# A spectral and MLP kernel on one core: group 0 normalized three quarters on VectorE, w1's first high half and three of its four low halves on GpSimd

## The chip, the core and the metric

The kernel runs on one core of a Trainium2 chip. The time is the device time of one execution in microseconds; the median of the runs shown is compared. The profile is that of one execution. Engines are named as the profile names them: PE is TensorE (PEld its weight loads), DVE is VectorE, ACT is ScalarE, POOL is GpSimd, SP issues the DMAs.

## What is computed

```python
def _A_ref(x, w_r, w_i):
    X = rfft2(x); X = X * (w_r + 1j * w_i)
    return irfft2(X, s=(S, D))

def _B_ref(x, w1, w2, w3, w4):
    h = _gelu(_layernorm(x) @ w1)
    # four quarters of h, shifted by +1, -1, +2, -2 tokens
    hs = concatenate([g0, g1, g2, g3], axis=-1) @ w2
    x1 = x + hs
    h2 = _gelu(_layernorm(x1) @ w3) @ w4
    return x1 + h2

xn = _layernorm(x)
return x + _A_ref(xn, A_w_r, A_w_i) + _B_ref(xn, B_w1, B_w2, B_w3, B_w4)
```

x is 2048 tokens by 448, w1 and w2 are 448 by 448, w3 is 448 by 1792 and w4 1792 by 448, all in float32.

## The kernel before

The tokens lie in 16 blocks of 128 partitions by 448 (`xb(b)`), which are worked in four groups of four (`GRP`; group 0 holds blocks 14, 15, 0, 1, and group 1 holds 2 to 5). Every large product is made of float16 halves: an operand is scaled by a power of two and split into a high half and a low half, and a product is three passes of matmuls, high by high, high by low and low by high (`PASS`).

The part that the change touches is the first 40 us or so. In program order it goes like this.

- TensorE runs 26 matmuls on zeros (`warm_up`) while the first loads come in. SP issues the loads in the order group 0's x, w1 in pieces, group 1's x, the rest of w1, w2, group 2's x and further weights.
- ACT sums the squares of w1 into `m1` (`squares`, L253).
- `norm1(0, ...)` makes the statistics of group 0's four blocks (`stats`: L306 and the aggregate L307), five small VectorE operations (L324 to L328, the last writes `nma`), and the first normalization of each block in place (L336, or L333 where it is ACT's). Its list names the engine of each block. It returns `refine`, ten small GpSimd operations in a chain (L343 to L352) whose last one writes `gsc`, the scale that the first GELU uses.
- `powers(m1, ...)` turns the sum of squares into two powers of two: a reduce (L258), a one-column matmul (L260), and VectorE's L262, L264, L266 (which gives the scale `s1`) and L267.
- `T1(0, [t])` transposes the four blocks' columns 128t to 128t + 127 on TensorE (L389), ACT copies the high half (L393) and VectorE subtracts for the low half (L394). Quarter 3 has 64 columns, and its high and low half lie on top of each other in one tile.
- `split_w` splits one quarter t of w1 (128 rows): ACT writes the scaled high half (L280) and VectorE the low half (L281). With `low` set to P, GpSimd first scales the quarter in place (L276), ACT copies the high half from it (L277) and GpSimd subtracts (L278). Before, quarters 0 and 1 go the first way and 2 and 3 the second.
- `w1_in` does the matmuls of w1 (L420): quarter 0 for all four blocks of group 0, quarter 1 for all four, then quarters 2 and 3 for the first two blocks. The last two blocks' quarters 2 and 3 come after `T1(1)` and after the matmul of `powers(m2, ...)`, the scale of w2.
- `norm1(1, ...)` does the same for group 1, with a list of what each of the four statistics is ordered behind.

The planner of the tile framework decides the order of the instructions on each engine ahead of time: it plays the program through with its own costs and takes, whenever an engine is free, the earliest instruction of the program that it holds to be ready. `behind(key)` holds an instruction back until those noted under `after[key]` have been issued. This holds for instructions of the same engine alone, and it is an order, not a wait. On the chip each engine then runs its list in order, and waits where data are late.

`w1s` is w1 as loaded, `w1p` its halves, `xT` the transposed halves, `xt` the x blocks, `w2s` and `w2p` the same for w2. L924 and L925, L470 and L863 are DMAs on SP further down; L462 is the split of the GELU's output, L478 the product with w2.

Of the kernel before, what the change touches and what calls it, by code (L numbers as in the profile page):

```python
# [15 lines left out]
AF = mybir.ActivationFunctionType  # L16
ALU = mybir.AluOpType
# [108 lines left out]
def body(tc, nc, x, wf, w1, w2, w3, w4, c_g, c_n, c_small, out):  # L126
    V, A, P, T, SY = nc.vector, nc.scalar, nc.gpsimd, nc.tensor, nc.sync
# [28 lines left out]
    def bank(tag, name):  # L156
        return ps.tile([128, 512], F32, tag=tag, bufs=2, name=name)
# [10 lines left out]
    def xb(b):  # L168
        return xt[b // 2][:, b % 2]
# [7 lines left out]
    def stage(name, n, side, dtype=F32):  # L177
        t = pw.tile([128, 1808], F32, tag=f"stage{side}", bufs=1, name=name)
        return (t if dtype is F32 else t.bitcast(dtype))[:, :n]
# [24 lines left out]
    w1s = stage("w1s", F, 0).rearrange("p (t n) -> p t n", t=4)  # L204
# [44 lines left out]
    def squares(col, src, junk=None):  # L249

        n = src.shape[-1]
        junk = xr.bitcast(F16) if junk is None else junk
        A.activation(out=junk[:src.shape[0], :n], in_=src, func=AF.Square, scale=2.0 ** -20, accum_out=col)  # L253

    def powers(m, n, key, tag="acc", spare=0):

        t = pc.tile([128, 2], F32, name=f"pt{key}")
        after["r" + key] = (V.tensor_reduce(out=t[:, 0:1], in_=m[:, :n], axis=AX.X, op=ALU.add).ins,)  # L258
        pm = bank(tag, f"pm{key}") if isinstance(tag, str) else tag
        i = T.matmul(pm[:, 0:1], ones, t[:, 0:1], start=True, stop=True)  # L260
        after["p" + key] = (i.ins,)
        V.tensor_scalar(out=t[:, 1:2], in0=pm[:, 0:1], scalar1=2.0 ** -58, scalar2=None, op0=ALU.max)  # L262
        e = pc.tile([128, 3], I32, name=f"pe{key}")
        V.tensor_scalar(out=e[:, 0:1], in0=t.bitcast(I32)[:, 1:2], scalar1=1, scalar2=0x7F800000,  # L264
                        op0=ALU.logical_shift_right, op1=ALU.bitwise_and)
        V.tensor_scalar(out=e[:, 1:2], in0=e[:, 0:1], scalar1=-1, scalar2=185 - spare << 23, op0=ALU.mult, op1=ALU.add)  # L266
        i = V.tensor_scalar(out=e[:, 2:3], in0=e[:, 0:1], scalar1=1, scalar2=69 + spare << 23, op0=ALU.mult, op1=ALU.add)  # L267
        after["e" + key] = (i.ins,)
        return e.bitcast(F32)[:, 1:2], e.bitcast(F32)[:, 2:3]
# [1 line left out]
    def absmax(out_, in_):  # L271
        V.tensor_reduce(out=out_, in_=in_, axis=AX.X, op=ALU.max, apply_absolute_value=True)

    def split_w(hi, lo, src, s, low=None):
        if low is P:
            after["ps"] = (P.tensor_scalar(out=src, in0=src, scalar1=s, scalar2=0.0, op0=ALU.mult, op1=ALU.add).ins,)  # L276
            i = A.activation(out=hi, in_=src, func=AF.Copy)  # L277
            j = P.tensor_tensor(out=lo, in0=src, in1=hi, op=ALU.subtract)  # L278
            return i.ins, j.ins
        i = A.activation(out=hi, in_=src, func=AF.Copy, scale=s)  # L280
        j = V.scalar_tensor_tensor(out=lo, in0=src, scalar=s, in1=hi, op0=ALU.mult, op1=ALU.subtract)  # L281
        return i.ins, j.ins

# [16 lines left out]
    def stats(src, key, mv=None, pins=None):  # L300
        if mv is None:
            mv = pc.tile([128, 4, 2], F32, tag="mv", bufs=3, name=f"mv{key}")
        for i, s in enumerate(src):
            st = pc.tile([128, 6], F32, tag="st", bufs=4, name=f"st{key}_{i}")
            with behind(*pins[i]) if pins else contextlib.nullcontext():
                V.bn_stats(out=st, in_=s)  # L306
            V.bn_aggr(out=mv[:, i, :], in_=st)  # L307
        return mv
# [10 lines left out]
    def norm1(g, apply, pins=None):  # L319

        bs, c = GRP[g], slice(4 * g, 4 * g + 4)
        mv, a, y, nm = mva[:, c], va[:, :, c], vy[:, :, c], nma[:, c]
        stats([xb(b) for b in bs], f"a{g}", mv, pins)
        V.tensor_scalar(out=a[:, 1], in0=mv[:, :, 1], scalar1=1.0 + EPS, scalar2=EPS * EPS, op0=ALU.mult, op1=ALU.add)  # L324
        V.tensor_scalar(out=a[:, 0], in0=mv[:, :, 1], scalar1=EPS, scalar2=None, op0=ALU.add)
        V.tensor_single_scalar(vyi[:, :, c], va.bitcast(I32)[:, :, c], 1, op=ALU.logical_shift_right)
        V.tensor_scalar(out=vyi[:, :, c], in0=vyi[:, :, c], scalar1=-1, scalar2=0x5F3759DF, op0=ALU.mult, op1=ALU.add)
        i = V.scalar_tensor_tensor(out=nm, in0=mv[:, :, 0], scalar=-1.0, in1=y[:, 1], op0=ALU.mult, op1=ALU.mult)  # L328
        after["c", g] = (i.ins,)
        for k, b in enumerate(bs):  # L330
            y_, m_ = y[:, 1, k:k + 1], nm[:, k:k + 1]
            if apply[k] is A:
                i = A.activation(out=xb(b), in_=xb(b), func=AF.Identity, scale=y_, bias=m_)  # L333
                after["na", g] = (i.ins,)
            else:
                i = apply[k].tensor_scalar(out=xb(b), in0=xb(b), scalar1=y_, scalar2=m_, op0=ALU.mult, op1=ALU.add)  # L336
                after["n" if apply[k] is V else "np", g] = (i.ins,)

        q, z = (pc.tile([128, 2, 4], F32, tag=f"v{t}", bufs=2, name=f"v{t}{g}") for t in "qz")
        w, r = vw[:, :, c], vr[:, :, c]  # L340

        def refine():
            P.tensor_tensor(out=q, in0=y, in1=y, op=ALU.mult)  # L343
            P.tensor_tensor(out=q, in0=q, in1=a, op=ALU.mult)
            P.tensor_scalar(out=w, in0=q, scalar1=-10.0 / 3.0, scalar2=None, op0=ALU.add)
            P.tensor_tensor(out=w, in0=w, in1=q, op=ALU.mult)
            P.tensor_scalar(out=w, in0=w, scalar1=5.0, scalar2=None, op0=ALU.add)
            P.tensor_tensor(out=z, in0=w, in1=w, op=ALU.mult)
            P.tensor_tensor(out=z, in0=z, in1=q, op=ALU.mult)
            P.tensor_scalar(out=z, in0=z, scalar1=-0.5 * 0.375 ** 3, scalar2=1.5 * 0.375, op0=ALU.mult, op1=ALU.add)  # L350
            P.tensor_tensor(out=r, in0=z, in1=w, op=ALU.mult)
            i = P.tensor_scalar(out=gsc[:, c], in0=r[:, 1], scalar1=r1, scalar2=None, op0=ALU.mult)  # L352
            after["g", g] = (i.ins,)
        return refine
# [17 lines left out]
    after = {}  # L372

    @contextlib.contextmanager
    def behind(*key):
        key = key if len(key) > 1 else key[0]
        with contextlib.ExitStack() as st:
            for i in after[key]:
                st.enter_context(tc.issue_after(i))
            yield  # L380
# [26 lines left out]
    w1p = p1.tile([128, 8, D], F16, name="w1p")  # L407
# [6 lines left out]
    def w1_in(g, units, ts, passes=range(3)):  # L414
        for p in passes:
            for t in ts:
                for i, pm in units:
                    wi, xi = ((0, 0), (0, 4), (4, 0))[p]
                    if t < 3 or p != 1:
                        m = T.matmul(pm[:, :D], xTs[g][:, xi + t, 128 * i:128 * i + 128], w1p[:, wi + t],  # L420
                                     start=t == 0 and p == 0, stop=t == 3 and p == 2)
        after["u"] = (m.ins,)
# [447 lines left out]
    def w4_split(f):  # L870
        split_w(w4p[0][:, 0, f:f + 2], w4p[0][:, 1, f:f + 2], w4raw(f, 2), s4)
# [1 line left out]
    for t in range(3):  # L873
        squares(m1[:, t:t + 1], w1s[:, t])
    squares(m1[:64, 3:4], w1s[:64, 3])
    n1 = [norm1(0, [P,V,P,V])]
    with behind("n", 0):
        s1, r1 = powers(m1, 4, "1", "mm")
    first = [bank("mm" if k < 2 else "sp", f"pw1_0{k}") for k in range(4)]
    for t in range(4):  # L880
        with behind("p1"):
            T1(0, [t])
        with behind("a0", t):
            after["w1", t] = split_w(w1p[:, t], w1p[:, 4 + t], w1s[:, t], s1, P if t > 1 else V)
    h1 = pc.tile([128, 1], F32, name="h1")
    V.tensor_scalar(out=h1, in0=s1, scalar1=2.0 ** -5, scalar2=None, op0=ALU.mult)
    for t in range(2):
        w1_in(0, list(enumerate(first)), [t])
    n = 2
    for unit in list(enumerate(first))[:n]:  # L890
        w1_in(0, [unit], [2, 3])
    with behind("ps"):
        n1[0]()
    n1.append(norm1(1, [P, V, A, V], [("r1",), ("a0", 0), ("w1", 0), ("w1", 1)]))
    with behind("w1", 3):
        squares(m2, flat(w2s))
    T1(1)
    with behind("T", "a1"):
        for unit in list(enumerate(first))[n:2]:
            w1_in(0, [unit], [2, 3])  # L900
    with behind("n", 1), behind("u"):
        s2, r2 = powers(m2, 1, "2", first[0][:, 448:512])
    with behind("p2"):
        for unit in list(enumerate(first))[2:]:
            w1_in(0, [unit], [2, 3])
    s12 = pc.tile([128, 4], F32, name="s12")
    V.tensor_tensor(out=s12[:, 0:1], in0=h1, in1=s2, op=ALU.mult)
    V.scalar_tensor_tensor(out=s12[:, 1:2], in0=r1, scalar=2.0 ** 5, in1=r2, op0=ALU.mult, op1=ALU.mult)
# [28 lines left out]
    with behind("a2"):  # L937
        n1 = [norm1(3, [P, P, P, P])]
# [169 lines left out]
```

## Time and profile before

| What | us |
|---|---|
| median of 3 runs | 408.12 (407.88 to 408.28) |
| the profiled execution | 408.05 |
| its span, first to last instruction | 406.3 |
| PE busy in the span | 399.9 |
| DVE busy | 333.6 |
| ACT busy | 255.1 |
| POOL busy | 100.4 |

TensorE's granted clock was 0.998 of full speed over the span. A line of the timeline gives the start and the length of a stretch of like instructions in microseconds, the engine, the line of the kernel, what is written and read, the shapes and the count; in brackets stands how long the engine sat idle before and what ended that. The ends of matmuls are modelled, so that the busy time of a matmul overlaps the next one's.

### The profile page before, as it was taken

What the parts mean: (1) busy time and instruction counts of PE and PEld (TensorE: products, weight loads), DVE (VectorE), ACT (ScalarE), POOL (GpSimd) and SP (SyncE); (2) the same over time, 40 slices, a digit from 0 to 9 for tenths busy, and PEclk for the clock granted to TensorE, in tenths of its full rate; (3) what the DMA queues carried; (4) which work ended last, traced back from release to release, by engine and by line L of the source; (5) the groups of instructions that cost most, each with busy time, mean ns of one, the idle gap of its engine ahead of it and who ended that gap; (6) DMA issues with size and microseconds to landing.
All of it is one profiled execution on the core that took longest, in us unless ns stands there. A gap on an engine that the chain in (4) does not pass through costs nothing.

```text
span 406.3 us, 8732 instructions
## 1 busy us (share of the span) xinstructions
PE 399.9 (98%) x3391; PEld 297.2 (73%) x3391; DVE 333.6 (82%) x702; ACT 255.1 (63%) x433; POOL 100.4 (25%) x158
## 2 busy tenths in 40 slices
PE   8999999999999999999999999999999999999996
PEld 3555555865667877777878878777677779998995
DVE  5898799898947887988698888965999999965645
ACT  4788889874568857655698878853354544353431
POOL 6859910111146946500021111110000000000000
PEclk9999999999999999999999999999999999999999
DMA  8978975567489661637256556510011023100101
GB/s 280 389 272 160 249 152 138 122 121 163 95 225 266 234 191 46 219 95 185 72 144 164 162 142 161 139 27 2 24 69 70 24 90 92 47 2 2 45 2 45
DMA packets 54596, 52.07 MB, mean 128 GB/s; under 512 B 35678, under 2 KB 48542, under 8 KB 54556
## 3 DMA queue, kind: packets, MB, share of 16 engines
q1 hardware_dynamic: 54556, 51.53, 46.0%
q8 instruction: 26, 0.43, 0.4%
q14 instruction: 14, 0.11, 0.1%
HBM read 38.28 MB, written 3.67 MB: 103 GB/s over the span
## 4 chain that ended last, share of the span: by engine, by line
PE 87%; POOL 5%; DMA 2%; DVE 2%; ACT 2%; issue 1%; SPq 0%; POOLq 0%; ACTq 0%
PE pw L400 33%; PE acc L808 23%; PE pw L478 6%; PE side L778 4%; PE acc L778 3%; PE pu L667 3%; PE ps L567 3%; PE pe L688 2%; PE pp L622 2%; PE px L639 2%; PE py L709 2%; PE pw L420 2%; DMA w1s<-w 1%; POOL xt L336 1%; DMA h<-x2mem 1%
## 5 line engine op out<-in xcount | busy, mean ns | idle before, releaser
L400 PE MATMUL pw<-x2mem,w3p 128*128 128x256 f16 x1232 | 151.3, 273 | 0.0
L400 PEld LDWEIGHTS <-w3p 128*128 128x128 f16 x1232 | 118.9, 98 | 19.3
L808 PE MATMUL acc<-w4p,hf 128*128 128x448 f16 (+1 forms) x516 | 104.4, 348 | 0.0
L808 PEld LDWEIGHTS <-hf 128*128 128x128 f16 x516 | 50.1, 98 | 37.6
L726 ACT ACTIVATE pw<-pw,pe 128x512 f32<-128x512 f32 x42 | 27.4, 654 | 26.8 <-PE pw L400 26.6
L729 DVE SCALAR_TENSOR_TENSOR hf<-pw,h,hf 128x512 f16<-128x512 f32 x42 | 31.3, 746 | 12.9 <-ACT hf L728 12.7
L478 PE MATMUL pw<-w2p,h 128*128 128x448 f16 x176 | 35.8, 353 | 0.9 <-DMA h<-x2mem 0.9
L420 PE MATMUL pw<-w1p,xT 128*128 128x448 f16 x176 | 34.9, 352 | 0.1
L648 POOL TENSOR_TENSOR z<-te 128x450 f32<-128x450 f32 x16 | 15.7, 983 | 70.8 <-DVE te L646 65.9
L728 ACT ACTIVATE hf<-pw,h 128x512 f16<-128x512 f32 x42 | 28.9, 687 | 5.0 <-PE acc L808 4.0
L478 PEld LDWEIGHTS <-h 128*128 128x128 f16 x176 | 17.0, 98 | 17.0 <-DMA h<-x2mem 2.0
L744 ACT ACTIVATE hz<-g,h 128x896 f16<-128x896 f32 x14 | 14.6, 1044 | 23.1 <-DVE g L741 23.1
L420 PEld LDWEIGHTS <-xT 128*128 128x128 f16 x176 | 17.1, 99 | 16.1 <-DVE xT L394 0.4
L778 PEld LDWEIGHTS <-hz 128*128 128x128 f16 x294 | 28.3, 98 | 0.6
L629 ACT ACTIVATE pf<-pp 64x450 f16<-64x450 f32 x32 | 17.4, 544 | 12.5 <-DVE pf L630 9.7
L630 DVE TENSOR_TENSOR pf<-pp,pf 64x450 f16<-64x450 f32 x32 | 19.9, 622 | 5.1 <-ACT pf L629 4.7
L745 DVE SCALAR_TENSOR_TENSOR hz<-g,h,hz 128x896 f16<-128x896 f32 x14 | 16.1, 1148 | 6.8 <-ACT hz L744 6.8
L550 POOL TENSOR_TENSOR f<-xr 128x452 f32<-128x452 f32 x16 | 19.7, 1251 | 0.6
L558 DVE TENSOR_TENSOR xh<-f,xh 128x452 f16<-128x452 f32 x16 | 14.3, 916 | 5.7 <-ACT xh L557 5.7
L644 ACT ACTIVATE te<-px 64x450 f32<-64x450 f32 x32 | 17.3, 541 | 1.2 <-PE px L639 0.6
L738 ACT ACTIVATE g<-pw,pe 128x512 f32<-128x512 f32 x14 | 9.6, 683 | 11.3 <-PE pw L400 11.3
L547 POOL TENSOR_TENSOR xr<-xf 128x452 f32<-128x452 f32 x8 | 9.2, 1156 | 22.3 <-issue 16.4
(188 smaller groups left out, 705.7 us busy)
## 6 DMA issues: line engine op xcount, KB each, us to landing
wc<-wf SPq DMA_DIRECT2D x32, 225.0 KB, 3.7
wl<-wf SPq DMA_DIRECT2D x8, 450.0 KB, 4.3
xt<-x SPq DMA_DIRECT2D x8, 448.0 KB, 7.1
xf<-x SPq DMA_DIRECT2D x8, 448.0 KB, 4.6
loads<-x SPq DMA_DIRECT2D x7, 448.0 KB, 4.0
out<-xt SPq DMA_DIRECT2D x13, 224.0 KB, 1.9
w3raw<-w SPq DMA_DIRECT2D x3, 896.0 KB, 10.8
gn<-c_g SPq DMA_DIRECT2D x16, 128.0 KB, 3.0
```

Source lines behind the costliest of these rows:

```text
L400: T.matmul(ps_out, wp[:, wi + t, cols], xT[:, xi + t, tok], start=t == 0 and wi + xi == 0, stop=t == 3 and wi == 4)
L420: m = T.matmul(pm[:, :D], xTs[g][:, xi + t, 128 * i:128 * i + 128], w1p[:, wi + t], start=t == 0 and p == 0, stop=t == 3 and p == 2)
L478: T.matmul(pm[:, :D], h[:, k], w2p[:, w], start=n == 0, stop=n == 10)
L550: P.tensor_tensor(out=f[:, :, k:k + 2].rearrange("p b s d -> p s b d"), in0=u[:, :, 0], in1=u[:, :, 1], op=op)
L629: A.activation(out=hi, in_=src, func=AF.Copy)
L630: V.tensor_tensor(out=lo, in0=src, in1=hi, op=ALU.subtract)
L644: A.activation(out=e[64 * h:64 * h + 64], in_=px_[64 - 64 * h:128 - 64 * h, :2 * DF], func=AF.Copy)
L726: A.activation(out=pm, in_=pm, func=AF.Gelu_apprx_tanh, scale=r3)
L728: i = A.activation(out=h[:, 0], in_=pm, func=AF.Copy, scale=h3)
L729: j = V.scalar_tensor_tensor(out=h[:, 1], in0=pm, scalar=h3, in1=h[:, 0], op0=ALU.mult, op1=ALU.subtract)
L778: m = T.matmul(to, h[:, hi, 128 * blk:128 * blk + 128], b[wi], start=new and n == 0, stop=n == 2 and (last if blk in (2, 5, 3, 0) else end ...
L808: m = T.matmul(to, h[:, hi, o:o + 128], w4p[0][:, wi, f, r], start=first and f % 2 == 0 and n == 0, stop=end and f % 2 == 1 and n == 2, sk ...
```

## The change

```diff
-    def split_w(hi, lo, src, s, low=None):
+    def split_w(hi, lo, src, s, low=None, high=None):
...
-        i = A.activation(out=hi, in_=src, func=AF.Copy, scale=s)
+        if high is P:
+            i = P.tensor_scalar(out=hi, in0=src, scalar1=s, scalar2=0.0, op0=ALU.mult, op1=ALU.add)
+        else:
+            i = A.activation(out=hi, in_=src, func=AF.Copy, scale=s)
...
-    n1 = [norm1(0, [P,V,P,V])]
+    n1 = [norm1(0, [P, V, V, V])]
...
-            after["w1", t] = split_w(w1p[:, t], w1p[:, 4 + t], w1s[:, t], s1, P if t > 1 else V)
+            after["w1", t] = split_w(w1p[:, t], w1p[:, 4 + t], w1s[:, t], s1, (V, P, P, P)[t], P if t in (0,) else A)
...
-    n = 2
-    for unit in list(enumerate(first))[:n]:
-        w1_in(0, [unit], [2, 3])
+    units = list(enumerate(first))
+    w1_in(0, [units[0]], [2, 3])
+    w1_in(0, [units[1]], [2, 3])
...
-    n1.append(norm1(1, [P, V, A, V], [("r1",), ("a0", 0), ("w1", 0), ("w1", 1)]))
+    n1.append(norm1(1, [P, V, A, V], [("e1",), ("a0", 0), ("w1", 0), ("w1", 1)]))
...
-    with behind("T", "a1"):
-        for unit in list(enumerate(first))[n:2]:
-            w1_in(0, [unit], [2, 3])
...
-        for unit in list(enumerate(first))[2:]:
-            w1_in(0, [unit], [2, 3])
+        w1_in(0, [units[2]], [2, 3])
+    with behind("p2"):
+        w1_in(0, [units[3]], [2, 3])
```

Group 0's third block is normalized on VectorE, no longer on GpSimd. The high half of w1's quarter 0 is written by GpSimd in place of ACT; its low half stays on VectorE. Quarter 1 goes the second way of `split_w`: GpSimd scales it, ACT copies the high half, GpSimd subtracts for the low half. Quarters 2 and 3 stay as they were. The first statistics of group 1 are ordered behind L267 (`e1`) in place of L258 (`r1`). The loops over the four blocks are written out; the loop removed from behind `T` and `a1` ran over nothing. The values computed are the same.

## The prediction

> **What bounds the kernel now.** I read four views, in this order: the page's totals and its chain, the waits of TensorE, the timeline of TensorE over the stretch that the change touches, and then the timelines of the engines that feed it there.
>
> ```profile
> PE 399.9 (98%) x3391; PEld 297.2 (73%) x3391; DVE 333.6 (82%) x702; ACT 255.1 (63%) x433; POOL 100.4 (25%) x158
> PE 87%; POOL 5%; DMA 2%; DVE 2%; ACT 2%; issue 1%; SPq 0%; POOLq 0%; ACTq 0%
> ```
>
> And of the waits of TensorE the two largest behind its start:
>
> ```profile
> PE pw L478 <- DMA h<-x2mem: 0.9, 3, 0.4
> PE pta L389 <- POOL xt L336: 0.7, 1, 0.7
> ```
>
> TensorE is busy for 98% of the span. The change leaves its matmuls as they are in number and size, so the time can move only by what TensorE idles, and there is little of that: the one wait that lies in the part the change rewrites is that of the transposes of group 1 (L389) for a block normalized on GpSimd (L336).
>
> ```profile
> 9.54 0.38 PE L260 MATMUL pm<-pt,ones 128*128 128x1 f32 x2 [0.37 <-DVE pt L258]
> 9.79 2.00 PE L389 MATMUL pta<-ident,xt 128*128 128x128 f32 x16
> 11.72 6.92 PE L420 MATMUL pw<-w1p,xT 128*128 128x448 f16 x34
> 19.30 1.97 PE L389 MATMUL pta<-ident,xt 128*128 128x128 f32 x16 [0.66 <-POOL xt L336]
> 21.24 10.37 PE L420 MATMUL pw<-w1p,xT 128*128 128x448 f16 x54
> 31.45 1.91 PE L389 MATMUL pta<-ident,xt 128*128 128x128 f32 x16
> 33.72 1.31 PE L478 MATMUL pw<-w2p,h 128*128 128x448 f16 x6 [0.36 <-DMA h<-x2mem]
> ```
>
> ```profile
> 16.73 0.49 PEld L420 LDWEIGHTS <-xT 128*128 128x128 f16 x4 [0.37 <-DVE xT L394]
> 17.54 0.66 PEld L420 LDWEIGHTS <-xT 128*128 128x128 f16 x4 [0.31 <-issue]
> ```
>
> The 54 matmuls from 21.24 take 10.37 us, the last of them about 0.35 of it, so one follows another after (10.37 - 0.35) / 53 = 0.189 us. At that pace the 34 from 11.72 would be through at 11.72 + 34 x 0.189 = 18.15, and the transposes begin at 19.30. So **1.15 us of TensorE time are lost between 11.72 and 19.30**. The weight loads say where: some 0.1 before 16.73 (a low half of the transposed x, L394), some 0.2 before 17.54, and 0.8 before 19.30. From 19.30 to 33.36 there is no gap at all. What the change can win directly is thus about 1.2 us, 0.3% of the time.
>
> **The change part by part.** These rows feed that stretch, GpSimd's first, then VectorE's and one of ScalarE's:
>
> ```profile
> 8.08 1.91 POOL L336 TENSOR_SCALAR xt<-xt,vy,nma 128x448 f32<-128x448 f32 x2 [2.57 <-DVE nma L328]
> 10.82 1.25 POOL L276 TENSOR_SCALAR w1s<-w1s,pe 128x448 f32<-128x448 f32 x2 [0.83 <-DMA w1s<-w]
> 12.04 0.20 POOL L343 TENSOR_TENSOR vq<-vy 128x8 f32<-128x8 f32 x1
> 12.32 0.70 POOL L344 TENSOR_TENSOR vq<-vq,va 128x8 f32<-128x8 f32 x1
> 15.04 1.04 POOL L278 TENSOR_TENSOR w1p<-w1s,w1p 128x448 f16<-128x448 f32 x1
> 16.45 1.03 POOL L278 TENSOR_TENSOR w1p<-w1s,w1p 128x448 f16<-128x448 f32 x1
> 17.75 0.33 POOL L352 TENSOR_SCALAR gsc<-vr,pe 128x4 f32<-128x4 f32 x1
> 18.30 0.94 POOL L336 TENSOR_SCALAR xt<-xt,vy,nma 128x448 f32<-128x448 f32 x1
> 19.21 0.33 POOL L344 TENSOR_TENSOR vq<-vq,va 128x8 f32<-128x8 f32 x1
> 21.73 0.30 POOL L352 TENSOR_SCALAR gsc<-vr,pe 128x4 f32<-128x4 f32 x1
> 24.03 0.64 POOL L276 TENSOR_SCALAR w2s<-w2s,pe 128x448 f32<-128x448 f32 x1 [2.00 <-ACT x2mem L460]
> 28.88 0.20 POOL L343 TENSOR_TENSOR vq<-vy 128x8 f32<-128x8 f32 x1 [2.36 <-DVE vy L327]
> ```
>
> ```profile
> 7.92 0.93 DVE L336 TENSOR_SCALAR xt<-xt,vy,nma 128x448 f32<-128x448 f32 x2
> 9.33 0.16 DVE L258 TENSOR_REDUCE pt<-m 128x1 f32<-128x4 f32 x1 [0.47 <-ACT xr L253]
> 9.40 0.62 DVE L306 BATCH_NORM_STATS2 sta<-xt 128x6 f32<-128x448 f32 x1
> 10.15 0.13 DVE L262 TENSOR_SCALAR pt<-pm 128x1 f32<-128x1 f32 x1
> 12.29 0.67 DVE L281 SCALAR_TENSOR_TENSOR w1p<-w1s,pe,w1p 128x448 f16<-128x448 f32 x1
> 14.09 0.66 DVE L281 SCALAR_TENSOR_TENSOR w1p<-w1s,pe,w1p 128x448 f16<-128x448 f32 x1
> 14.66 0.62 DVE L306 BATCH_NORM_STATS2 sta<-xt 128x6 f32<-128x448 f32 x1
> 16.92 0.58 DVE L324 TENSOR_SCALAR va<-mva 128x4 f32<-128x4 f32 x1
> 18.02 0.16 DVE L328 SCALAR_TENSOR_TENSOR nma<-mva,vy 128x4 f32<-128x4 f32 x1
> ```
>
> ```profile
> 11.01 0.66 ACT L280 ACTIVATE w1p<-w1s,pe 128x448 f16<-128x448 f32 x1
> ```
>
> 1. *Group 0 normalized [P, V, V, V].* VectorE gets a third L336. Two take 0.93, so three take about 1.36 and end near 9.29, inside the 0.47 that VectorE idles before L258 at 9.33. GpSimd loses one of its two. Its first must be there for the first transpose at 9.79; two took until 9.99 with the third transpose waiting a trace for the second. Cost between -0.1 and +0.1; I take 0. The cover is that idle 0.47: without it L258 and the scale s1 behind it would be late by 0.43.
> The row shows what the two engines do to each other: GpSimd's two L336 take 1.91 together, although a GpSimd operation of that kind (L276) needs 0.62. The Trainium skill's page "SBUF — State Buffer" (Who interferes with whom) says that such a VectorE instruction and GpSimd exclude one another for a whole instruction. By that rule GpSimd's one block is held until the third L336 ends and is ready near 9.7; by the rows' pace alone it would be ready at about 9.0. Both are before 9.79, and the sum is the same.
>
> 2. *First statistics of group 1 behind L267 in place of L258.* At 9.40 the statistics (0.62) and an aggregate sit in front of L262, which starts at 10.15, though the matmul it reads ends at 9.54 + 0.38 = 9.92. L262 can move to about 9.97 and s1 with it: -0.18. GpSimd's work on w1, now from 10.82, then starts at 10.64.
>
> 3. *w1's first high half on GpSimd.* ACT's 0.66 at 11.01 ends at 11.67, and the first matmul starts at 11.72; the transposes alone would allow 11.63. On GpSimd the operation isn't in the trace; the nearest rows are L276 (0.62, one input) and L278 (1.04, two inputs and the same f16 output). I take 0.64, since it has one input: ready at 11.3, or 11.7 by the other end. Gain 0.1, at least 0.
>
> 4. *Low half of the second quarter from VectorE to GpSimd.* VectorE loses 0.57 (14.09 to 14.66). GpSimd gains a scaling (0.62) and a subtraction (1.04); with the high half that is 2.3 us more between 10.6 and 17.5, where it has no idle time now. From 10.64: high half 0.64 and three scalings 1.86 make 13.14; 0.5 for the time in which L281 holds GpSimd up (L344 took 0.70 beside it, where L343 took 0.20); three L278 make 16.8; one to three of the small operations of L343 to L352, 0.28 each, come between. The last low half is ready between 16.4 (no hold-up, one small operation) and 17.8; I take 17.2, against 17.48 now. TensorE reaches the first matmul that needs it, the 30th, at 11.63 + 29 x 0.189 = 17.11. Wait 0.1 instead of 0.2 (0 to 0.7), and the 34 matmuls end at 17.2 + 5 x 0.189 = 18.2, at worst 18.8.
> The Trainium skill's page "GPSIMD Engine Reference" (Engine selection) advises against this step: two-input elementwise work is about twice as slow there as on VectorE. The rows give 1.04 against 0.66. Where that would tell is the rival "GpSimd late" below.
>
> 5. *The gap before group 1's transposes.* L328 ends at 18.18, and both GpSimd's L336 (18.30, 0.94) and the transposes follow. VectorE has no wait in its timeline between 12.29 and 18.18, so its 0.57 come off: 17.6. If L324, which takes 0.58 beside the L278 at 16.45 and where its neighbour L328 takes 0.16, is no longer held, 0.4 more: 17.2. GpSimd is free from 17.2. L336 then runs from about 17.4 to 18.3, and the transposes start at **18.4 against 19.30: -0.9** (18.3 to 18.9, that is -1.0 to -0.4). What is then late next is gsc (L352), which ends at 18.08 now and about 20 then; only the first GELU needs it, and that feeds nothing on TensorE before 31.
>
> 6. *Does it last?* The next thing that GpSimd owes is w2's scaling at 24.03; before it GpSimd idles for 2.00, and behind it 2.36 before 28.88. Of the 2.3 us that it gets, some 1.5 are still there at 22.03 (end of the second L352): 23.5, still before 24.03. The transposes at 31.45 wait for blocks that depend on work that moves along. Splitting the loop over the last two units only names each apart. I take 0 for all this, between -0.3 and +0.5 (part of the 0.9 us of waits for h, more or less).
>
> The sum is -0.9, in which steps 1 to 4 are contained, since the start at 18.4 takes the place of all that went before. The profiled execution took 408.05 us, 1.75 outside its span; 408.05 - 0.9 = 407.15. The median of the runs is 0.07 higher: **407.2 us**.
>
> **The rivals.**
>
> *VectorE waits for x (slower).* The last of group 1's statistics is ordered behind the second quarter's VectorE subtraction. That subtraction goes to GpSimd, and an order holds within one engine only, so nothing keeps this statistic back any more. Its x comes late:
>
> ```profile
> L201 SPq DMA_DIRECT2D xt<-x x1: 432/432/432, 4.3 to 4.3; - x1
> DMA to landing us min/median/max: 6.7/6.7/6.7
> ```
>
> It lands near 11.0. If the planner puts the statistic into VectorE's free time before L262, L262 starts at 11.0 + 0.6 = 11.6 in place of 10.0, and everything behind s1 is 1.6 later: -0.9 + 1.6 gives 408.8. In front of L258 (2.2 later) it gives 409.4. I take 409.1. For it: nothing but the planner's own guess of the landing stands in the way. Against it: the planner would have to believe in a landing more than 1 us too early. It decides from the moment that L306 for this block stands in front of L262.
>
> *GpSimd late (slower).* If the planner puts group 1's block behind the whole chain L343 to L352 (10 operations, 0.3 each, as the stretch from 19.21 to 22.03 shows), L336 starts at 16.8 + 3.0 = 19.8 and the transposes at 20.7: 1.4 late, 409.5; the last two units' ten matmuls, 1.9 us, cover this if they are put first. For it: GpSimd has no idle time there. Against it: in the rows of before, L336 at 18.30 stands ahead of the L344 of a chain already begun. It decides when L336 starts after 18.2.
>
> *Absorbed.* TensorE is 0.9 earlier at 31.45 and waits it out for group 2's blocks or for h at 33.72: 408.1. For it: three waits for h are already there. Against it: their causes shift too.
>
> **How the numbers follow.** The forecast 0.50, with its own range 406.7 to 407.7; absorbed 0.13; VectorE waits 0.15; GpSimd late 0.22. A difference of 0.2%, 0.8 us, is about what a measurement of this kernel tells from none. Of the forecast's half, four fifths lie below 407.3: faster 0.41 with a little of "absorbed"; the rest of both, and covered cases of the last rival, 0.22 within; slower 0.37. The range from 406.6 (all of 1.15 and 0.3 of the waits for h) to 409.5 (the last rival) leaves under 0.2 outside.
>
> **What would show it.** Group 1's first transpose near 18.4; no L306 between L258 and L262, and L262 near 10.0; the first matmul near 11.6; L278 for the last quarter ending near 17.2; the wait "pta from POOL xt" below 0.3; PE's busy time unchanged. Wrong if the transposes start after 19.3, if L262 starts after 10.2, or if new waits of TensorE turn up between 22 and 55.

## The result and the profile after

The changed kernel takes **408.64 us** (median of 20 runs, 408.44 to 410.18) against 408.12 before: a ratio of 1.0015, interval 1.0008 to 1.0021. It is slower by 0.15%: a small change, inside the band called no change, but clear of the scatter and the other way than forecast. It is 1.4 us above the forecast. Its profiled execution took 408.59, 406.80 of them in the span (before 408.05 and 406.34).

The page's totals and the chain, then the waits of TensorE (microseconds in total, times, longest). In the views below, rows that the argument does not need are left out.

```profile
PE 399.7 (98%) x3391; PEld 297.3 (73%) x3391; DVE 332.9 (82%) x702; ACT 254.5 (63%) x432; POOL 101.3 (25%) x160
PE 87%; POOL 6%; DMA 3%; issue 1%; SPq 1%; ACT 1%; DVE 0%; POOLq 0%
```

```profile
PE pta L392 <- POOL xt L339: 0.9, 1, 0.9
PE pw L481 <- ACT x2mem L463: 0.7, 1, 0.7
PE pw L481 <- DMA h<-x2mem: 0.5, 2, 0.3
```

The work is the same; the waits are not. The wait for group 1's block (L339, before L336; from L306 to L889, lines have moved by 3) was to shrink from 0.7 and grew to 0.9. The wait at the first product with w2 (L481, before L478) was 0.36 and is 0.75. The view names ScalarE's L463 as its releaser, a copy that ends at 34.22; but in the kernel before the same copy (L460, 33.26 to 33.89) was still running when the product started at 33.72, so the product does not need it. What ends the wait is the landing of h: the product follows the issue of that DMA by 3.04 in both kernels. TensorE's timeline:

```profile
9.81 0.38 PE L260 MATMUL pm<-pt,ones 128*128 128x1 f32 x2 [0.44 <-DVE pt L258]
11.84 6.68 PE L423 MATMUL pw<-w1p,xT 128*128 128x448 f16 x34
19.42 1.97 PE L392 MATMUL pta<-ident,xt 128*128 128x128 f32 x16 [0.90 <-POOL xt L339]
21.37 10.38 PE L423 MATMUL pw<-w1p,xT 128*128 128x448 f16 x54
34.24 1.31 PE L481 MATMUL pw<-w2p,h 128*128 128x448 f16 x6 [0.75 <-ACT x2mem L463]
```

The transposes of group 1 start at 19.42, where 19.30 was before and 18.4 was forecast; the first product with w2 at 34.24 against 33.72. That 0.52 stays to TensorE's last group of matmuls (398.28 before, 398.80 after; span +0.46). Where it arises shows in GpSimd's and VectorE's timelines:

```profile
8.24 1.22 POOL L339 TENSOR_SCALAR xt<-xt,vy,nma 128x448 f32<-128x448 f32 x1 [2.73 <-DVE nma L331]
10.88 0.64 POOL L281 TENSOR_SCALAR w1p<-w1s,pe 128x448 f16<-128x448 f32 x1 [1.42 <-DVE pe L267]
15.02 2.03 POOL L278 TENSOR_TENSOR w1p<-w1s,w1p 128x448 f16<-128x448 f32 x2
17.67 0.23 POOL L350 TENSOR_SCALAR vw<-vw 128x8 f32<-128x8 f32 x1
17.99 0.42 POOL L346 TENSOR_TENSOR vq<-vy 128x8 f32<-128x8 f32 x1
18.41 0.95 POOL L339 TENSOR_SCALAR xt<-xt,vy,nma 128x448 f32<-128x448 f32 x1
21.19 0.30 POOL L355 TENSOR_SCALAR gsc<-vr,pe 128x4 f32<-128x4 f32 x1
```

```profile
8.10 1.61 DVE L339 TENSOR_SCALAR xt<-xt,vy,nma 128x448 f32<-128x448 f32 x3
9.62 0.14 DVE L258 TENSOR_REDUCE pt<-m 128x1 f32<-128x4 f32 x1
10.23 0.16 DVE L262 TENSOR_SCALAR pt<-pm 128x1 f32<-128x1 f32 x1 [0.47 <-PE pm L260]
17.64 0.16 DVE L331 SCALAR_TENSOR_TENSOR nma<-mva,vy 128x4 f32<-128x4 f32 x1
17.84 0.94 DVE L339 TENSOR_SCALAR xt<-xt,vy,nma 128x448 f32<-128x448 f32 x2
20.75 1.29 DVE L397 TENSOR_TENSOR xT<-pta,xT 128x512 f16<-128x512 f32 x2 [1.91 <-ACT xT L396]
29.98 1.88 DVE L465 SCALAR_TENSOR_TENSOR x2mem<-pw,h,x2mem 128x224 f16<-128x224 f32 x5
```

And VectorE before the change, at the two ends of the same stretch:

```profile
20.24 0.81 DVE L462 SCALAR_TENSOR_TENSOR x2mem<-pw,h,x2mem 128x224 f16<-128x224 f32 x2 [0.70 <-POOL vw L346]
20.97 0.68 DVE L394 TENSOR_TENSOR xT<-pta,xT 128x512 f16<-128x512 f32 x1
...
29.46 1.88 DVE L462 SCALAR_TENSOR_TENSOR x2mem<-pw,h,x2mem 128x224 f16<-128x224 f32 x5
```

Three things are to be seen. **The start is late:** VectorE now has three L339, and they take 1.61 (the two of before took 0.93). L258 follows them without the idle time it had, at 9.62 instead of 9.33, and GpSimd starts on w1 at 10.88, where 10.64 was forecast. **GpSimd's block is late:** nma is there at 17.80, but L339 starts at 18.41, behind an L346 that takes 0.42 where the one at 13.71 takes 0.20. **VectorE restarts late:** before, the first block's split (L462, 0.81) began in VectorE's wait for the transposes. It needs gsc and the GELU behind it; gsc now ends at 21.49 instead of 18.08, so VectorE idles 1.91 instead of 0.70 and restarts at 20.75 with the split still to do. That restart, with the first low half (L397), is 1.33 behind the start of the transposes; before, the split stood there already at 0.94, so some 0.4 of its 0.81 lay in the wait. From its restart to the split that the first h needs, VectorE's timeline shows no single idle time over 0.2, in both kernels.

The path from there can be written as a sum. SP issues the transposing DMA of the first h (L473, before L470) at 30.68 before and 31.20 after, and the first product with w2 follows 3.04 later in both. SP's queue, before and then after:

```profile
30.68 1.34 SPq L470 DMA_TRANSPOSE h<-x2mem  x1
31.20 1.34 SPq L473 DMA_TRANSPOSE h<-x2mem  x1
```

So the product's start is the start of group 1's transposes + the time to VectorE's restart + VectorE's full stretch to that issue + 3.04:

- before: 19.30 + 0.94 + 10.44 + 3.04 = 33.72
- after: 19.42 + 1.33 + 10.45 + 3.04 = 34.24

The late gsc costs 0.39, in the second term. The first term, which should have been 0.9 smaller, is 0.12 larger.

### The profile page after: what moved, and what is told of

Its sections match the earlier page's. It is cut to its first block, busy times and chain, and to the rows that moved or that the text cites. A ratio compares the mean times of both kernels' runs of the same rounds, so it can differ in the third digit from the quotient of the medians.

```text
span 406.8 us, 8730 instructions
## 1 busy us (share of the span) xinstructions
PE 399.7 (98%) x3391; PEld 297.3 (73%) x3391; DVE 332.9 (82%) x702; ACT 254.5 (63%) x432; POOL 101.3 (25%) x160
## 4 chain that ended last, share of the span: by engine, by line
PE 87%; POOL 6%; DMA 3%; issue 1%; SPq 1%; ACT 1%; DVE 0%; POOLq 0%
PE pw L403 33%; PE acc L811 23%; PE pw L481 6%; PE side L781 4%; PE acc L781 3%; PE pu L670 3%; PE ps L570 3%; PE pe L691 2%; PE pp L625 2%; PE px L642 2%; PE py L712 2%; PE pw L423 2%; DMA w1s<-w 2%; POOL xt L339 1%; DMA h<-x2mem 1%
## 5 line engine op out<-in xcount | busy, mean ns | idle before, releaser
L481 PE MATMUL pw<-w2p,h 128*128 128x448 f16 x176 | 35.8, 353 | 1.3 <-ACT x2mem L463 0.7
L481 PEld LDWEIGHTS <-h 128*128 128x128 f16 x176 | 17.0, 98 | 17.4 <-DMA h<-x2mem 2.4
L423 PEld LDWEIGHTS <-xT 128*128 128x128 f16 x176 | 17.2, 99 | 15.7 <-DVE xT L397 0.4
L632 ACT ACTIVATE pf<-pp 64x450 f16<-64x450 f32 x32 | 17.4, 543 | 12.5 <-DVE pf L633 9.7
L560 ACT ACTIVATE xh<-f 128x452 f16<-128x452 f32 x16 | 8.7, 573 | 9.7 <-POOL f L553 8.0
```

The source lines that it names most:

```text
L481: T.matmul(pm[:, :D], h[:, k], w2p[:, w], start=n == 0, stop=n == 10)
```

## The experiments

Two theories were tested. **"Late start"**: the third normalization on VectorE holds L258, and so w1's scale and GpSimd's queue. **"Full VectorE"**: the path from group 1's transposes to the first h goes through VectorE's unbroken stretch; a late gsc takes the split out of VectorE's gap, so that VectorE restarts later with as much to do, and work put into the gap shortens the stretch. The expectations of e1 to e4 call an earlier form of this "late gsc". The rival is the prediction's own: gsc feeds nothing on TensorE before 31, VectorE has room, and what TensorE gains at the transposes lasts.

The times up to the product with w2 are from the timeline of one profiled execution; the median, the ratio and the span (its median) are over the runs. "VectorE restarts" is its first split or low half behind the start of group 1's transposes, and "stretch" is from there to the first issue of h. Each ratio is against runs of the kernel before taken beside that kernel: their medians are 408.12 for the changed kernel, 407.92 for e1 to e4, 408.15 for e5 to e8 and 408.17 for e9 to e12, the medians of their spans 406.2, 406.4 and 406.5 for e1 to e12.

| kernel | L258 | group 1's transposes | VectorE restarts | first h issued | stretch | product with w2 | median | ratio [interval] | span |
|---|---|---|---|---|---|---|---|---|---|
| before | 9.33 | 19.30 | 20.24 | 30.68 | 10.44 | 33.72 | 408.12 | | 406.2 to 406.5 |
| after | 9.62 | 19.42 | 20.75 | 31.20 | 10.45 | 34.24 | 408.64 | 1.0015 [1.0008, 1.0021] | 406.8 |
| e1 | 9.30 | 19.15 | 20.47 | 30.98 | 10.51 | 34.02 | 408.52 | 1.0017 [1.0008, 1.0026] | 406.7 |
| e2 | 9.20 | 18.75 | 20.07 | 30.60 | 10.53 | 33.63 | 408.52 | 1.0013 [1.0004, 1.0022] | 406.3 |
| e3 | 9.48 | 19.73 | 20.62 | 31.12 | 10.50 | 34.17 | 408.49 | 1.0016 [1.0007, 1.0025] | 406.8 |
| e4 | 9.44 | 19.74 | 21.06 | 31.82 | 10.76 | 38.55 | 413.98 | 1.0151 [1.0137, 1.0165] | 412.0 |
| e5 | 9.59 | 19.48 | 20.43 | 30.87 | 10.44 | 33.90 | 408.95 | 1.0021 [1.0012, 1.0029] | 407.2 |
| e6 | 9.79 | 19.58 | 20.91 | 30.13 | 9.22 | 33.17 | 407.85 | 0.9991 [0.9982, 1.0000] | 405.7 |
| e7 | 9.46 | 19.00 | 20.44 | 29.64 | 9.20 | 32.67 | 407.59 | 0.9989 [0.9980, 0.9998] | 405.6 |
| e8 | 9.66 | 19.75 | 20.70 | 31.66 | 10.96 | 35.30 | 408.48 | 1.0008 [1.0000, 1.0017] | 406.7 |
| e9 | 9.34 | 19.41 | 20.74 | 31.50 | 10.76 | 34.53 | 409.29 | 1.0035 [1.0023, 1.0048] | 407.5 |
| e10 | 9.76 | 19.60 | 20.93 | 31.20 | 10.27 | 34.24 | 408.60 | 1.0016 [1.0007, 1.0025] | 406.5 |
| e11 | 9.77 | 19.67 | 20.98 | 30.35 | 9.37 | 33.38 | 407.64 | 0.9992 [0.9983, 1.0001] | 405.7 |
| e12 | 9.18 | 18.73 | 20.17 | 29.52 | 9.35 | 32.55 | 408.44 | 1.0011 [1.0002, 1.0020] | 406.3 |

Two things have to be kept in mind. The loads do not land at the same time in every execution: with two normalizations on VectorE, L258 stands anywhere between 9.18 and 9.77, so a few tenths between two rows of the first columns are not by themselves an effect of the edit. And the time outside the span differs between the kernels (last section), so that a median can be higher where the span is not. The product with w2 follows the issue of h by 3.03 to 3.05 in all rows but e4 (6.73) and e8 (3.64).

**e1: the changed kernel, group 0's chain (gsc) ahead of GpSimd's work on w1.**

```diff
+    n1[0]()
...
-    with behind("ps"):
-        n1[0]()
```

> The changed kernel with group 0's chain of ten small GpSimd operations (L346 to L355, the last writes gsc) put ahead of GpSimd's work on w1. Theory 'late gsc' (gsc at 21.5 in place of 18.1 moves the first GELU behind the transposes of group 1, VectorE's split of it out of an idle slot into a full stretch, and so h and the wait at 34 by 0.5): gsc before 16, first GELU near 18.5, the product with w2 starts at 33.8 or earlier, time 408.1 or below. Rival 'late start' (VectorE's third normalization holds up L258 and with it everything by 0.1 to 0.3): 408.6, no change. Rival 'transposes of group 1' (they set the time, 0.1 late): only as far as these move.

gsc was ready at 13.13 and the first GELU began at 18.75, but the product with w2 came at 34.02 and the median was 408.52: the expectation was missed, since VectorE's gap stayed empty. ScalarE's timeline and VectorE's:

```profile
20.34 0.63 ACT L463 ACTIVATE x2mem<-pw,h 128x448 f16<-128x448 f32 x1
```

```profile
20.47 0.69 DVE L397 TENSOR_TENSOR xT<-pta,xT 128x512 f16<-128x512 f32 x1 [1.08 <-ACT xT L396]
21.08 0.80 DVE L465 SCALAR_TENSOR_TENSOR x2mem<-pw,h,x2mem 128x224 f16<-128x224 f32 x2
```

The planner now puts ScalarE's copy L463, which the split reads, behind its first L396. An early gsc is not enough: the split has to be in the gap, and here it isn't, so that VectorE restarts 1.32 behind the transposes, as with a late gsc.

**e2: the changed kernel, group 0 back at two and two.**

```diff
-    n1 = [norm1(0, [P, V, V, V])]
+    n1 = [norm1(0, [P, V, P, V])]
```

> The changed kernel with group 0's third block back on GpSimd ([P, V, P, V]); the order on TensorE and ScalarE stays. 'Late gsc': gsc and the first GELU stay where they are within 0.3, time 408.6. 'Late start': L258 starts 0.1 to 0.3 earlier and the time falls with it to 408.3 or below.

```profile
11.59 1.68 PE L423 MATMUL pw<-w1p,xT 128*128 128x448 f16 x8
...
18.75 1.97 PE L392 MATMUL pta<-ident,xt 128*128 128x128 f32 x16
...
33.63 1.31 PE L481 MATMUL pw<-w2p,h 128*128 128x448 f16 x6 [0.81 <-ACT x2mem L463]
```

The late start is gone: the last sum over w1 is through at 9.17 and L258 follows at 9.20, where in the changed kernel the sum was through at 9.11 and L258 came at 9.62. At the transposes that is 0.67: they start at 18.75, 0.55 ahead of before. TensorE's weight load still waits 0.49 there for GpSimd's block, which is through at 18.70. The product with w2 is only 0.09 ahead, for the time to VectorE's restart is 1.32 (before 0.94), gsc ending at 20.95. GpSimd's timeline shows how 0.4 at the start became 0.67:

```profile
10.46 0.64 POOL L281 TENSOR_SCALAR w1p<-w1s,pe 128x448 f16<-128x448 f32 x1 [0.51 <-DVE pe L267]
...
17.57 0.20 POOL L346 TENSOR_TENSOR vq<-vy 128x8 f32<-128x8 f32 x1
17.76 0.94 POOL L339 TENSOR_SCALAR xt<-xt,vy,nma 128x448 f32<-128x448 f32 x1
```

Here L346 starts before VectorE's two L339 (17.68) and takes 0.20. In the changed kernel it comes at 17.99, behind the start of the first of them (17.84; the two take 0.94, so the first lasts to about 18.3), and it takes 0.42 and ends at 18.41. The Trainium skill's page "SBUF — State Buffer" (Who interferes with whom) says that such a VectorE instruction, where it comes first, blocks GpSimd for the whole of it; these two rows agree.

The median, 408.52, did not fall as "late start" expected, though the span did, by 0.5 to 406.3: more time lies outside the span (last section).

**e3: the changed kernel, the second quarter's low half back on VectorE. e4: the first quarter's high half back on ScalarE.**

```diff
-  (V, P, P, P)[t], P if t in (0,) else A)
+  (V, V, P, P)[t], P if t in (0,) else A)     # e3
+  (V, P, P, P)[t], A)                         # e4
```

> The changed kernel with the low half of w1's second quarter back on VectorE (its high half on ACT then), the first high half still on GpSimd. GpSimd loses 1.66 us before gsc, VectorE gets 0.6 back. 'Late gsc': gsc near 19.8, time between 408.0 and 408.4. 'Late start': 408.6.

> The changed kernel with the first high half back on ACT, the low half of the second quarter still on GpSimd. GpSimd loses 0.64 us before gsc. 'Late gsc': gsc near 20.9, still behind the transposes of group 1, time 408.4 to 408.6. 'Late start': 408.6.

In e3 gsc is early again (18.19) and VectorE restarts 0.89 behind the transposes, but these start 0.31 later than in the changed kernel: the low half is worth about what its cost in gsc is, and the time is the same. The 408.0 to 408.4 expected by "late gsc" were missed. e4 tells nothing about its one operation, since the planner gave TensorE another order behind 32; it is taken up under the hardware below.

**e5: the kernel before, with [P, V, V, V] alone.** The order on TensorE and ScalarE is that of before.

```diff
-    n1 = [norm1(0, [P,V,P,V])]
+    n1 = [norm1(0, [P,V,V,V])]
```

> The kernel before with one part of the change: group 0 normalized [P, V, V, V]. 'Late start' (the third L336 on VectorE takes 0.7 in place of the 0.43 predicted and puts L258 behind it by 0.2 to 0.4, and all that follows is late by as much): span 0.2 to 0.4 above that of before. 'Late gsc' or 'full VectorE' alone: no difference, within 0.1.

```profile
8.06 1.60 DVE L336 TENSOR_SCALAR xt<-xt,vy,nma 128x448 f32<-128x448 f32 x3
9.59 0.14 DVE L258 TENSOR_REDUCE pt<-m 128x1 f32<-128x4 f32 x1
```

VectorE takes 1.60 for its three blocks, as in the changed kernel (1.61), and L258 is right behind. The transposes and the product with w2 are 0.18 later than before. Over the runs the kernel loses more than was expected, 0.80 in the median (408.95 against 408.15) and 0.8 in the span. What is lost behind 34 the profile names only in pieces: TensorE is 0.15 late from 51 to 239 and 0.42 late from 240 on, with a new wait of 0.18 there for VectorE's L645. What this edit costs in all is therefore not explained.

**e6, e7: group 2's first two statistics in VectorE's gap**, that is behind the second L258; e6 is the changed kernel with this alone, e7 has [P, V, P, V] as well.

```diff
-    with behind("a1"):
-        n1.append(norm1(2, [P, V, A, P], [("e2",), ("e2",), ("e2",), ("e2",)]))
+    n1.append(norm1(2, [P, V, A, P], [("r2",), ("r2",), ("e2",), ("e2",)]))
```

> The changed kernel with the statistics of group 2's first two blocks taken forward, from behind L267 of the second scale to behind the second L258, where VectorE idles 1.1 to 1.9 us. 'Full VectorE' (from its restart behind the transposes of group 1 to the split that the first h needs, VectorE has 10.4 us of work without a break in every kernel, so h comes 10.4 after the restart): h comes 0.8 to 1.2 earlier, the product with w2 starts 0.7 to 0.9 earlier (then right behind the transposes of group 2), span near 406.0 against 406.8. Rival 'ACT or the wrap DMA sets h': span 406.6 or more.

> The same with group 0 back at [P, V, P, V]. 'Full VectorE' and 'late start' both: the two gains add, span near 405.5 (406.3 with the block back alone, less 0.8). If only 'late start' holds: 406.3. If the time outside the span is again 2.15 (as in the kernel with the block back alone) the median is 0.35 above what the span says.

VectorE in e6, then TensorE in e7:

```profile
18.92 1.14 DVE L309 BATCH_NORM_STATS2 sta<-xt 128x6 f32<-128x448 f32 x2
19.98 0.30 DVE L310 BATCH_NORM_AGGREGATE mva<-sta 128x2 f32<-128x6 f32 x2
20.91 1.29 DVE L397 TENSOR_TENSOR xT<-pta,xT 128x512 f16<-128x512 f32 x2 [0.63 <-ACT xT L396]
```

```profile
19.00 1.97 PE L392 MATMUL pta<-ident,xt 128*128 128x128 f32 x16
...
32.67 1.31 PE L481 MATMUL pw<-w2p,h 128*128 128x448 f16 x6
```

1.14 us of statistics go into the gap, and the stretch shrinks by 1.2 (10.45 to 9.22 and 9.20). The first h is issued 1.07 earlier than in the changed kernel in e6, 1.56 in e7. No wait is listed any more at the first product with w2, which now stands behind twelve of group 2's sixteen transposes; a new one follows behind it, for a copy of w2p (0.47 at 35.76 in e6, 0.38 at 35.17 in e7). With the changed kernel's own parts left in, e6 is 0.8 us below it (1.1 in the span), and **e7, at 407.59, is below both kernels**, by a ratio of 0.9989 to the kernel before.

**e8, e11: the kernel before, with one (e8) and with two (e11) of those statistics in the gap.** Each line stands in place of the two removed in e6.

```diff
+    n1.append(norm1(2, [P, V, A, P], [("r2",), ("e2",), ("e2",), ("e2",)]))   # e8
+    n1.append(norm1(2, [P, V, A, P], [("r2",), ("r2",), ("e2",), ("e2",)]))   # e11
```

> The kernel before with the statistics of group 2's first block taken forward in the same way; VectorE idles 0.7 there. 'Full VectorE': h 0.5 to 0.7 earlier, the product with w2 0.35 earlier (then the transposes of group 2 are in front of it), span 0.3 to 0.5 below that of before. Rival: no change, within 0.1.

> The kernel before, with the first two statistics of group 2 in VectorE's gap; the planner leaves SP's order as it is (the first h ahead of the two copies of w2p), unlike the version with one statistic. Full VectorE: group 2's chain ends at 27.5 to 28.0, the first h is issued at 29.5 to 30.2, the first product with w2 comes at 32.6 to 33.3, the median is 407.3 to 407.7. If what was late in the version with one statistic was not SP's order but the h path itself: first h again at 31 or later, and 408.1 to 408.6.

e8 was a miss: group 2's nma was there 1.05 earlier (27.94 against 28.99), and so were the splits behind it (28.40 against 29.46), but h was issued later. SP's queue shows why:

```profile
30.41 0.52 SPq L924 DMA_DIRECT2D w2p<-w2p  x1
31.02 0.54 SPq L923 DMA_DIRECT2D w2p<-w2p  x1
31.66 4.38 SPq L470 DMA_TRANSPOSE h<-x2mem  x3
```

Two copies of w2p stand ahead of the first h, which in the kernel before are issued behind it (32.13 and 32.71). In e11 they are behind it again, h is issued at 30.35, and the median is 407.64, although the profiled execution started 0.44 late (L258 at 9.77). Its interval, 0.9983 to 1.0001, just reaches no change; its span is 0.8 below that of before. So the gap is worth about as much without the change as with it.

**e9: the kernel before, with a late gsc alone.**

```diff
-    with behind("ps"):
-        n1[0]()
...
+    with behind("np", 1):
+        n1[0]()
```

Group 1's `norm1` also moves up in the program, ahead of these lines.

> The kernel before, with group 0's chain (L343 to L352, gsc) behind group 1's block, so that the first GELU comes about 2.5 us later; the normalizations and all of w1's work stay. Full VectorE: the two splits of the first unit, 0.8 us, leave VectorE's gap before its restart at 20.24 and are added behind it; the transposes of group 1 stay at 19.3 (19.0 to 19.5), the first h is issued 0.4 to 0.9 later than 30.68, the first product with w2 comes at 34.1 to 34.6, the median is 408.5 to 409.0. Prediction's step 5 (gsc feeds nothing on TensorE before 31, and VectorE has room): first product with w2 at 33.7 within 0.2, 408.1 within 0.2.

Both chains now run side by side behind the block, so gsc comes near 23.6, later than in the changed kernel (21.49). ScalarE's timeline, then VectorE's:

```profile
23.62 1.66 ACT L459 ACTIVATE pw<-pw,gsc 128x448 f32<-128x448 f32 x3 [1.48 <-POOL gsc L352]
```

```profile
20.74 1.29 DVE L394 TENSOR_TENSOR xT<-pta,xT 128x512 f16<-128x512 f32 x2 [1.08 <-ACT xT L393]
```

The transposes start at 19.41, as before within 0.11. VectorE restarts 1.33 behind them instead of 0.94, its stretch is 0.32 longer, and the product with w2 is 0.81 late. That is what full VectorE expected, and the prediction's step that a late gsc costs nothing is wrong. The median, 409.29, is a little beyond what was expected.

**e10: the kernel before, with the second quarter's low half on GpSimd alone.**

```diff
-  split_w(..., P if t > 1 else V)
+  split_w(..., P if t > 0 else V)
```

> The kernel before, with the low half of w1's second quarter on GpSimd and nothing else of the change. GpSimd's order in it has part of group 0's chain ahead of the subtractions, and gsc behind group 1's block. Full VectorE: the transposes of group 1 start at 18.6 to 19.2, earlier than 19.30, since VectorE is 0.57 shorter; VectorE's work behind them still ends no earlier, so the first product with w2 is at 33.4 to 34.2 and the median 407.8 to 408.6. Prediction's steps 4 to 6 (the gain lasts): the product with w2 is as much earlier as the transposes, 33.0 to 33.3, and the median 407.4 to 407.7.

The profiled execution began 0.43 late (L258 at 9.76, behind the last sums over w1), which hides part of the gain, so the transposes are measured from the first matmul with w1: 19.60 - 12.09 = 7.51 against 19.30 - 11.72 = 7.58. No gain to speak of. GpSimd's timeline says why:

```profile
18.19 0.20 POOL L349 TENSOR_TENSOR vz<-vz,vq 128x8 f32<-128x8 f32 x1
18.39 1.16 POOL L336 TENSOR_SCALAR xt<-xt,vy,nma 128x448 f32<-128x448 f32 x1
```

The block starts at 18.39, behind pieces of both chains, and takes 1.16 beside VectorE. gsc ends at 20.92, VectorE restarts 1.33 behind the transposes. The central part of the change, alone, gives 1.0016: it buys nothing at the transposes. What it pays for gsc is not seen in the span, whose median, 406.5, is that of before beside it; the 0.43 in the median time lies outside the span (2.16 against 1.72).

**e12: e7, with group 1's chain behind group 1's block.**

```diff
-    n1[1]()
+    with behind("np", 1):
+        n1[1]()
```

> The changed kernel with group 0 back at [P, V, P, V], two statistics of group 2 in VectorE's gap, and group 1's chain (gsc) behind group 1's block. Full VectorE: against the same kernel without the last edit (transposes 19.00, product 32.67, 407.59) L339 starts behind nma at once: transposes of group 1 at 18.4 to 18.7, and since the gap is filled the gain lasts: product with w2 at 32.1 to 32.5, 407.1 to 407.4. If VectorE is still what bounds there: transposes earlier, product at 32.6 to 32.8, 407.6 within 0.2.

```profile
18.73 1.97 PE L392 MATMUL pta<-ident,xt 128*128 128x128 f32 x16
...
32.55 1.31 PE L481 MATMUL pw<-w2p,h 128*128 128x448 f16 x6
...
78.02 4.33 PE L481 MATMUL pw<-w2p,h 128*128 128x448 f16 x22 [0.61 <-DMA h<-x2mem]
```

The transposes come 0.27 earlier than in e7, the product with w2 0.12. Both are within 0.05 of what was expected, and the time is not (408.44, where 407.1 to 407.4 was expected): 0.61 are lost at 78, where the planner's other order lets TensorE wait for another h. e7 stays the one with the lowest median.

## Why the prediction was wrong

Two of the three signs of being wrong that the prediction names came: the transposes start after 19.3 (19.42) and L262 after 10.2 (10.23). In place of the third, a new wait of TensorE between 22 and 55, an old one grew: that at the first product with w2, from 0.36 to 0.75.

**Step 1 (third normalization, cost 0).** This failed in size and in cover. Three L339 take 1.61, so the third costs 0.68, not 0.43. (GpSimd's one block was through at 9.46, between the 9.0 and the 9.7 of the prediction, and held nothing up.) The cover, 0.47, was one execution's: it ends when the last sums over w1 are through, and L258 stands between 9.18 and 9.77 with the loads alone (e12, e11, both with two on VectorE). In all six kernels with three on VectorE the profile shows no idle time ahead of L258. In the changed kernel ScalarE's last sum over w1 was through at 9.11, so L258 could have stood near 9.15; it lost almost 0.5, of which the comparison with the kernel before, whose loads came later, shows 0.29.

**Steps 2 to 4** were right in direction. L262 follows its matmul at once (0.42 behind the start of pm, before 0.61); the first matmul follows pm by 2.03 instead of 2.18, and in e2, with the start mended, stands at 11.59 (forecast 11.63). The last low half is ready at 17.05 (forecast 17.2).

**Step 5 (transposes at 18.4)** failed. nma at 17.80 is close to the 17.6 that was worked out. But "GpSimd is free from 17.2" left out four small operations of the chains that follow the last low half (L348, L349, L350 and L346), the last of them held up by VectorE's own L339, so the block starts at 18.41. This is the rival "GpSimd late" in mechanism and in its mark (start after 18.2), though four small operations did it, not the whole chain. e2 shows that 0.67 of it hung on the late start: there the transposes start at 18.75. What is left to 18.4 has two causes that end together: the block, which starts at 17.76 where about 17.4 was forecast and is through at 18.70, and TensorE's 34 matmuls, which begin at 11.59 with waits for w1 and x on the way and are through at 18.71, not at 18.2.

**Steps 5 and 6 (gsc late, no cost; the gain lasts).** This is the step that would have failed even with the transposes in time. gsc feeds nothing on TensorE before 31, but by way of the GELU it feeds a split that stood in VectorE's gap, and VectorE's stretch behind that gap is what the first h waits for. The price in the changed kernel is 0.39. e9, with a late gsc alone, shows the same 0.39 at the restart, and 0.32 more in the stretch, gsc being later there; in e10 a stretch shorter by 0.17 makes up for part of it. With the forecast's 18.4 the sum is 18.4 + 1.33 + 10.45 + 3.04 = 33.22: at best 0.5 of the 0.9 would have arrived. The view that would have told is VectorE's timeline from 19 to 31, where one idle time is followed by ten microseconds without another; the prediction read VectorE only up to 18.

So the miss at the product with w2, 34.24 - (33.72 - 0.90) = 1.42, is, by the profiled executions, 0.67 of late start and its collision, 0.35 of a block and matmuls that were not as early as forecast even without it, and 0.39 of gsc. "VectorE waits for x" did not occur: no L309 stands between L258 and L262. "Absorbed" named the right place, the wait for h, but not the cause: at this place a gain does move along (e2 against the changed kernel: transposes 0.67 earlier, product 0.61; e7 against e6: 0.58 and 0.50). It is gsc that takes from it.

## What to carry to other kernels

Before an operation is moved onto an engine "with room", follow the result that it delays until a bounding engine's queue is reached: a small result that comes late can move another engine's work out of an idle slot into its full stretch. Of an engine that is 82% busy, look for the longest stretch without idle time and for the gap ahead of it; filling that gap gained 0.8 us on top of the changed kernel (e6) and 0.5 on top of the kernel before (e11), where the whole change lost 0.5. An idle time that ends with a load is cover only as large as the load is late, and one execution doesn't show by how much that varies.

## What the hardware showed unexpectedly

**Time outside the span.** It is steady for one kernel and differs between kernels: over the runs of each, its median is 1.81 after, 1.73 in e3, 1.80 in e5, but 2.16 in e2 and e10 and 2.14 in e6 and e12, within 0.1 to either side; that of before is 1.71 or 1.72. So e2's span, 406.3 in the median, is within 0.1 of that of the kernel before beside it (406.2), and its time is 0.6 longer (408.52 against 407.92). The cause stays open.

**A clock that falls behind an idle time.** e4's TensorE waited 1.00 up to 34.81, worked for 1.5, and waited 2.23 up to 38.55. The windows of e4 (length, then busy time and count of PE, PEld, DVE, ACT, POOL, then granted clock, DMA share and GB/s):

```profile
36.40:38.40 2.00, 0.00 (x0) 0.00 (x0) 1.94 (x5) 1.97 (x4) 2.00 (x2) 1.00 1.17 190
38.40:40.00 1.60, 1.45 (x6) 0.73 (x7) 1.60 (x4) 1.60 (x2) 1.34 (x5) 0.72 1.04 187
40.00:42.00 2.00, 2.00 (x7) 0.79 (x6) 1.35 (x10) 0.01 (x1) 1.64 (x9) 0.50 0.89 199
42.00:44.00 2.00, 2.00 (x10) 0.95 (x9) 0.10 (x1) 0.58 (x1) 2.00 (x7) 0.87 1.04 226
```

After the wait the granted clock falls to 0.50 and comes back in the course of the last of these windows. The matmuls in between (39.14 to 42.50) follow one another by 0.37 to 0.38 us, where 0.19 is usual. The two waits (3.23 together; the changed kernel waits 0.75 there) and the nine intervals at half pace (about 1.7 lost) make up most of the 4.8 us by which e4's profiled span is longer than the changed kernel's. The Trainium skill's page "TensorE: Matmul & The Clock Gate" (The HAM clock gate) gives half rate after an idle window of some 3.4 us; here a wait of 2.23 was enough, while e8's wait of 1.31 up to 35.30 left the clock at 1.00. Whether the wait of 1.00 ahead of it played a part is not shown.
